# Scores of a windowed attention by halves of the queries, on quarters of the matrix array

## The chip, the cores and the metric

The kernel runs on one core of a Trainium2 chip. The metric is the device time of one execution in microseconds (us): 638.39 as the median of three runs before the change (638.38 to 638.89). Six actors matter. TensorE multiplies matrices, with a row PE for its matmuls and a row PEld for its weight loads. VectorE (DVE), ScalarE (ACT) and GpSimd (POOL) do the elementwise work, and SyncE (SP) issues the transfers from HBM. Each engine takes its instructions in the order in which they were written; semaphores join them.

## The reference, cut to what matters

Attention over 2 batches, 8 heads, 768 positions, heads 64 wide, where a query sees the first 4 positions and the last 128; then two layers over 1536 tokens:

```python
scores = scale * np.matmul(q, k.transpose(0, 1, 3, 2))
keep = is_sink | in_window          # pos < n_sink, or 0 <= rel < window
a = softmax(np.where(keep, scores, -1e9))
x = np.matmul(a, v)                 # then heads side by side: 1536 x 512
h = x @ w_in;  g = P(h) / (Q(h) + 1e-6);  x = g @ w_out      # rational layer
h = np.maximum(x @ w_in2, 0.0);  out = h * h @ w_out2         # squared relu
```

The weights come as 64-bit numbers, and the kernel takes them apart into 32-bit ones itself.

## The kernel before, in words

**Units and steps.** Attention runs over 12 units of 128 queries (6 blocks of positions in each of 2 batches). A unit has 8 heads, which go in 4 pairs; a pair is one step n of `step(n)`, so there are 48 steps. The two heads of a pair lie one above the other on the 128 partitions (64 each), so their score matmuls use the upper and the lower half of the array's rows.

**Scores.** `scores(n)` (L373 to L399) is called for two steps at once, every second step. A block of queries after the first of its batch (10 of the 12 units) needs the keys of its own block and of the one before. `keys` holds four slots of 136 columns: 128 keys of a block and 8 sink keys. For each head one matmul (L382) of 64 rows, 128 queries and 2 x 136 = 272 columns writes a bank of PSUM. In the profile each such 32-bit matmul is two instructions, so a call for two steps is eight of them (x8). The first block of a batch has 128 columns instead. VectorE then replaces the part of the own block that lies ahead of the query by the block before (`copy_predicated`, L387), adds the mask and takes the maximum (L394, tile `ns`, running maximum `nmax`). ScalarE takes the exponential into `pe` (L411) and adds it up into `rs`.

**Behind the scores.** Step n also transposes the probabilities of step n-2 (L431), copies them out of PSUM (`pc`, L439, ScalarE) and splits them by the diagonal (GpSimd, `ph`). It multiplies those of step n-4 by the values (`pv`, L471, tile `O`). Once a unit the probabilities of the sinks are gathered (`sk`), transposed (`sinks_t`, L454), cast to `st` (L457 on ScalarE, L458 on VectorE) and multiplied by the sink values (L478, L479), after which VectorE scales the unit's result to `x` (L482). `sums` turns `rs` into its reciprocal. `xt` transposes `x` (L353) and splits it in two parts (L497, L498). Between these, VectorE takes weights apart (L241, L247, L253).

**Zeros.** `fill(d, m)` issues m matmuls of zeros, 512 columns wide (L512), whose result nobody reads. `NW0` (14) stand at the start, and `DENSE` says how many stand ahead of the scores of some steps: 22 more, 36 in all.

**Order.** The order of each engine is the order in which `step` calls these functions; nothing rearranges it. The last four steps are laid between the first slots of the two layers, whose matmuls (L597, L676) fill the rest of the time. PSUM tiles rotate: `S` and `T` have two buffers each, `O` and `U` one.

Of the kernel before, what the change touches and what calls it, by code (L numbers as in the profile page):

```python
# [15 lines left out]
P = 128  # L16
SK = 8
# [1 line left out]
TWO32 = 4294967296.0  # L19
WS = 3  # L20
NW0 = 14
DENSE = {0: 4, 2: 4, 4: 3, 6: 3, 24: 2, 26: 2, 28: 2, 30: 2}
QP = 1.0 + 1e-6

LEAST = 2.0 ** -15 * 1.125
# [12 lines left out]
def kernel(  # L38
# [24 lines left out]
    UPC = CT // P  # L63
    scale = 1.0 / float(D) ** 0.5
    BS = P + SK
    NS = 4

    cst = ctx.enter_context(tc.tile_pool(name="cst", bufs=1))
    ctx.enter_context(tc.manual_schedule())
# [33 lines left out]
    def setup_first(m_0):  # L103
        ta, tb = [
            wr.tile([P, DM, 2], I32, tag="wr", name="su", bufs=NWR).rearrange("p n t -> p (n t)") for _ in range(2)
        ]
        it, it2 = ta[:, 0:2 * P], ta[:, 2 * P:3 * P]
        rel, col = ta[:, 4 * P:6 * P].bitcast(F32), ta[:, 6 * P:7 * P].bitcast(F32)
        win, snk, tmp, ge = (
            tb[:, a:b].bitcast(F32) for a, b in ((0, 2 * P), (2 * P, 3 * P), (3 * P, 4 * P), (4 * P, 6 * P))  # L110
        )
        rf, neg = tb[:, 6 * P:6 * P + 4].bitcast(F32), tb[:, 6 * P + 4:6 * P + 6].bitcast(F32)
        nc.gpsimd.iota(it, pattern=[[-1, 2 * P]], base=P, channel_multiplier=1)
        nc.gpsimd.iota(it2, pattern=[[1, P]], base=0, channel_multiplier=0)
        nc.vector.tensor_copy(rel, it)
        nc.vector.tensor_copy(col, it2)
        nc.vector.tensor_scalar(out=ge, in0=rel, scalar1=0.0, scalar2=None, op0=ALU.is_ge)
        nc.vector.tensor_copy(rf, raw)
        rv = rf.rearrange("p (j w) -> p j w", w=2)
        nc.vector.tensor_scalar(out=neg, in0=rv[:, :, 0], scalar1=0.0, scalar2=TWO32, op0=ALU.is_lt, op1=ALU.mult)  # L120
        nc.vector.scalar_tensor_tensor(out=nw, in0=rv[:, :, 1], scalar=TWO32, in1=neg, op0=ALU.mult, op1=ALU.add)
        nc.vector.tensor_tensor(out=nw, in0=nw, in1=rv[:, :, 0], op=ALU.add)
        yield
        window = lambda x: nc.vector.scalar_tensor_tensor(
            out=win[:, x], in0=rel[:, x], scalar=nw[:, 1:2], in1=ge[:, x], op0=ALU.is_lt, op1=ALU.mult
        )
        window(slice(P, 2 * P))
        nc.vector.scalar_tensor_tensor(
            out=tmp, in0=col, scalar=nw[:, 0:1], in1=win[:, P:], op0=ALU.is_lt, op1=ALU.max
        )  # L130
        addm(m_0, tmp)
        yield
        window(slice(0, P))
        nc.vector.tensor_scalar(out=snk[:, 0:SK], in0=col[:, 0:SK], scalar1=nw[:, 0:1], scalar2=None, op0=ALU.is_lt)
        yield rel, win, snk, tmp

    def setup_rest(rel, win, snk, tmp, m_1, m_2, tri):
        def addm_s(dst, src):
            nc.scalar.activation(out=dst, in_=src, func=ACTF.Identity, scale=BIG, bias=nbig)

        nc.vector.tensor_scalar(out=tri, in0=rel[:, P:], scalar1=0.0, scalar2=None, op0=ALU.is_lt)
        nc.gpsimd.tensor_tensor(out=tmp, in0=win[:, 0:P], in1=win[:, P:], op=ALU.add)
        nc.gpsimd.tensor_tensor(out=win[:, P:P + SK], in0=snk[:, 0:SK], in1=win[:, 0:SK], op=ALU.subtract)
        yield
        addm_s(m_1[:, 0:P], tmp)
        nc.scalar.activation(out=win[:, P:P + SK], in_=win[:, P:P + SK], func=ACTF.Relu)
        addm_s(m_1[:, P:], win[:, P:P + SK])
        yield
        addm_s(m_2[:, 0:P], tmp)
        addm_s(m_2[:, P:], snk[:, 0:SK])  # L150

    def setup_moe():
        nc.scalar.mul(out=na, in_=ab[:, 0:4], mul=-1.0)
# [138 lines left out]


    def attention(ap, extra):
        keys = ap.tile([P, NPR, NS, BS], F32, name="keys")
        m_0 = ap.tile([P, P], F32, name="m_0")
        m_1, m_2 = (ap.tile([P, 160], F32, name=f"m_{j}")[:, 0:BS] for j in (1, 2))
        tri = ap.tile([P, P], I32, name="tri")
# [3 lines left out]
        def load(u, what="qkv"):  # L302
            b, i = divmod(u, NB)
            for nm, src in (("q", q), ("k", k)):
                if nm in what:
                    t = keys[:, :, u % NS, 0:P] if nm == "k" else ap.tile([P, NPR, P], F32, name="qr", bufs=3)
                    nc.sync.dma_start(
                        out=t, in_=src[b, :, :, i * P:(i + 1) * P].rearrange("(r e) d t -> (e d) r t", e=2)
                    )
                    ld[u, nm] = t  # L310
            if "v" in what:
                t = ap.tile([P, H, D], F32, name="vr", bufs=5)
                nc.sync.dma_start(out=t, in_=v[b, :, i * P:(i + 1) * P, :].rearrange("h p d -> p h d"))
                ld[u, "v"] = t
# [42 lines left out]

        def sink_keys(u):
            nc.gpsimd.tensor_copy(
                keys[:, :, :, P:], keys[:, :, u % NS, 0:SK].unsqueeze(2).to_broadcast([P, NPR, NS, SK])  # L360
            )

        def geom(u):

            i, s = u % NB, u % NS
            if i == 0:
                return slice(s, s + 1), P, m_0, 0, None
            m = m_1 if i == 1 else m_2
            if s == 0:
                return slice(0, NS, NS - 1), BS, m, 0, BS  # L370
            return slice(s - 1, s + 1), BS, m, BS, 0

        def scores(n):  # L373
            u, pr = divmod(n, NPR)
            slots, bw, mask, co, po = geom(u)
            w = bw if po is None else 2 * bw
            t = ps_s()
            d = [t[:, e] for e in range(2)]
            fill(d[0], DENSE.get(n, 0))
            for e in range(2):  # L380
                s = slice(D * e, D * e + D)
                nc.tensor.matmul(  # L382
                    d[e][:, 0:w].rearrange("p (j n) -> p j n", n=bw),
                    lhsT=ld[u, "q"][s, pr, :], rhs=keys[s, pr, slots, 0:bw], start=True, stop=True,
                )
            if po is not None:
                nc.vector.copy_predicated(  # L387
                    out=t[:, :, co:co + P], mask=tri.unsqueeze(1).to_broadcast([P, 2, P]), data=t[:, :, po:po + P]
                )
            ns = []  # L390
            for e in range(2):
                ix = u * H + 2 * pr + e
                t = ap.tile([P, 160], F32, name="ns", bufs=6)
                nc.vector.tensor_tensor_reduce(  # L394
                    out=t[:, 0:bw], in0=d[e][:, co:co + bw], in1=mask, scale=-scale, scalar=3.0e38,
                    op0=ALU.add, op1=ALU.min, accum_out=nmax[:, ix:ix + 1],
                )
                ns.append(t)
            kps[n] = ns  # L399

        def expo(n):
            u, pr = divmod(n, NPR)
            w = geom(u)[1]
            if pr == 0:
                pe_t[u] = ap.tile([P, NPR, 2, BS], F32, name="pe", bufs=2)
                rs_t[u] = ap.tile([P, 32], F32, name="rs", bufs=3)[:, 0:H]
            rs, t = rs_t[u], pe_t[u][:, pr]
            ns = kps.pop(n)
            for e in range(2):
                ix = u * H + 2 * pr + e  # L410
                nc.scalar.activation(  # L411
                    out=t[:, e, 0:w], in_=ns[e][:, 0:w], func=ACTF.Exp, scale=-1.0,
                    bias=nmax[:, ix:ix + 1], accum_out=rs[:, 2 * pr + e:2 * pr + e + 1],
                )
            pr_t[n] = t

        def sinks(n):
            u = n // NPR
            t = pe_t.pop(u)
            if u % NB and n % NPR == NPR - 1:  # L420
                sk[u] = ap.tile([P, 2, H, SK], F32, name="sk", bufs=2)
                nc.gpsimd.tensor_copy(
                    sk[u], t[:, :, :, P:].rearrange("p r e s -> p (r e) s").unsqueeze(1).to_broadcast([P, 2, H, SK])
                )

        def trans(n):
# [1 line left out]
            t = pr_t.pop(n)  # L428
            d = ps_t(tail=n >= NP - 2)
            for e in range(2):  # L430
                nc.tensor.transpose(d[:, e * P:(e + 1) * P], t[:, e, 0:P], ident)  # L431
            h = mp.tile([P, CT], F32R, tag=("gh", "gl")[n % 2], name="ph", bufs=2)
            h = h.bitcast(F32).rearrange("p (j e t) -> p j e t", j=2, e=2)
            dv = d[:, 0:2 * P].rearrange("p (e t) -> p e t", e=2)
# [83 lines left out]
        load(0, "v")  # L518
        load(1, "v")
        nc.sync.dma_start(out=ab, in_=coefs.partition_broadcast(P))  # L520
        fill(ps_t("T"), NW0)
        masks = setup_first(m_0)
        next(masks)
        next(masks)
# [2 lines left out]
        def step(n):  # L527
# [4 lines left out]
            if n == 0:  # L532
                scores(0)
                scores(1)
                rest = setup_rest(*next(masks), m_1, m_2, tri)
                next(rest)
                sink_keys(0)
            elif n % 2 == 0 and n < NP:
                scores(n)
                scores(n + 1)  # L540
            if 0 < n < 4:
                next(rest, None)
            if n == 2:
# [9 lines left out]
                trans(n - 2)  # L553
            if 0 <= n - 1 < NP and pr == 0:
                sinks(n - 1)
            if (n >= 6 and pr == 2 and n < NP) or n == NP + 1:
                sinks_t(n // 4 - 1)
                sums(n // 4 - 1)
            if 12 <= n <= NP and pr == 0:
                xt(n // 4 - 3)  # L560
            if n == NP + 1:
                xt(NU - 2)
            if 0 <= n - 4 < NP:
                pv(n - 4)
            if n == NP - 2:
                g1(0)
            if pr == 2 and u % NB == 0 and 0 < u < NU:
# [522 lines left out]
```

## Time and profile before

| | us |
|---|---|
| median of three runs | 638.39 |
| profiled execution | 638.53 |
| its span, first to last instruction | 636.8 |
| TensorE busy in the span | 625.2 (98%) |
| VectorE, ScalarE, GpSimd busy | 423.3, 356.6, 339.0 |

The span is 1.7 us shorter than the profiled execution's own time. Attention takes about the first 112 us of it. A busy matmul row counts from the start of a matmul to its modelled end, so that matmuls overlap; what TensorE's work costs is read from the distances between starts, as the chain of waits gives them.

### The profile page before, as it was taken

The page shows a single profiled execution, that of the slowest core. Times are in us where ns is not written, and L with a number is a line of the kernel's source. Part 1 is how long each engine was busy: PE and PEld are TensorE (multiplying, and loading weights), DVE is VectorE, ACT ScalarE, POOL GpSimd, SP SyncE. Part 2 cuts the span into 40 slices and gives each one's busy share as a digit, 9 for nine tenths or more (in the row PEclk, how much of TensorE's full clock was granted, in tenths as well). Part 3 has the DMA queues.
Part 4 walks back from the last instruction along what each step waited for, and adds up shares of the span by engine and source line. Part 5 has one row for each costly group of instructions (what it writes and reads, how often), then busy time and mean ns, then how long its engine had stood idle before and what let it go on. Part 6 is the DMA issues. An engine that isn't in the chain of part 4 may idle for free.

```text
span 636.8 us, 9037 instructions
## 1 busy us (share of the span) xinstructions
PE 625.2 (98%) x3060; PEld 514.7 (81%) x3060; DVE 423.3 (66%) x862; ACT 356.6 (56%) x772; POOL 339.0 (53%) x343
## 2 busy tenths in 40 slices
PE   8999999999999999999999999999999999999995
PEld 6788787888888888888888888888888888888884
DVE  4887884679888888777677779869594433441321
ACT  4777877778888788697778633333242222222220
POOL 3666865667767577586567557444443132222221
PEclk9999999999999999999999999999999999999999
DMA  8846820033223233201111148737556264420101
GB/s 214 251 128 180 226 71 31 1 99 100 83 84 100 66 100 99 67 33 34 33 46 55 35 136 259 245 115 243 191 166 231 69 221 123 173 76 1 66 1 72
DMA packets 64373, 72.03 MB, mean 113 GB/s; under 512 B 15424, under 2 KB 55360, under 8 KB 64320
## 3 DMA queue, kind: packets, MB, share of 16 engines
q1 hardware_dynamic: 64176, 71.38, 36.1%
q8 instruction: 26, 0.43, 0.3%
q14 instruction: 27, 0.22, 0.1%
q10 hardware_dynamic: 144, 0.00, 0.0%
HBM read 68.23 MB, written 3.15 MB: 112 GB/s over the span
## 4 chain that ended last, share of the span: by engine, by line
PE 92%; DVE 3%; ACT 3%; issue 1%; POOL 0%; DVEq 0%; ACTq 0%
PE s L676 41%; PE T L597 34%; PE U L597 7%; PE O L471 3%; PE s L382 3%; PE T L431 1%; DVE ns L394 1%; PE T L512 1%; ACT pe L411 1%; PE s L512 1%; PE O L478 1%; DVE s L387 0%; ACT pc L439 0%; ACT xf L497 0%; PE O L479 0%
## 5 line engine op out<-in xcount | busy, mean ns | idle before, releaser
L597 PE MATMUL T<-xh,w 128*128 128x512 f32 x640 | 210.4, 390 | 0.0
L659 POOL TENSOR_TENSOR gl<-g,gh 128x512 fp32r<-128x512 f32 x48 | 62.1, 1294 | 158.0 <-ACT gh L658 157.9
L597 PEld LDWEIGHTS T<-xh,w 128*128 128x128 f32 x640 | 120.2, 188 | 25.0
L676 PE MATMUL s<-gh,w 128*128 128x512 f32 x384 | 126.3, 390 | 0.0
L597 PE MATMUL T<-xl,w 128*128 128x512 f32 x320 | 124.5, 389 | 0.0
L676 PE MATMUL s<-w,gh 128*128 128x512 f32 x384 | 118.1, 389 | 0.0
L618 POOL TENSOR_TENSOR t<-t,ah 128x512 f32<-128x512 f32 x48 | 62.3, 1297 | 41.8 <-ACT t L615 35.9
L275 POOL TENSOR_TENSOR w<-wx,w 128x512 fp32r<-128x512 f32 x64 | 82.7, 1292 | 3.2 <-ACT w L274 3.0
L676 PEld LDWEIGHTS s<-gh,w 128*128 128x128 f32 x384 | 72.1, 188 | 15.0
L676 PEld LDWEIGHTS s<-w,gh 128*128 128x128 f32 x384 | 72.1, 188 | 14.9
L659 POOL TENSOR_TENSOR gl<-t,gh 128x512 fp32r<-128x512 f32 x48 | 62.3, 1297 | 38.0 <-ACT gh L658 35.1
L658 ACT CAST gh<-g 128x512 fp32r<-128x512 f32 x48 | 29.9, 623 | 82.4 <-PE s L676 77.0
L676 PE MATMUL s<-gl,w 128*128 128x512 f32 x192 | 74.7, 389 | 0.0
L676 PE MATMUL s<-w,gl 128*128 128x512 f32 x192 | 74.7, 389 | 0.0
L597 PEld LDWEIGHTS T<-xl,w 128*128 128x128 f32 x320 | 60.1, 188 | 12.3
L647 DVE SCALAR_TENSOR_TENSOR t<-t,U 128x512 f32<-128x512 f32 x48 | 33.0, 687 | 35.9 <-ACT U L644 35.6
L658 ACT CAST gh<-t 128x512 fp32r<-128x512 f32 x48 | 29.8, 622 | 37.6 <-DVE t L651 29.3
L632 DVE TENSOR_TENSOR g<-r,T 128x512 f32<-128x512 f32 x32 | 21.8, 683 | 42.8 <-ACT r L622 42.8
L622 ACT ACTIVATE r<-T 128x512 f32<-128x512 f32 x32 | 19.1, 598 | 53.2 <-PE T L597 53.1
L471 PE MATMUL O<-vr,ph 128*128 128x64 f32 x352 | 44.6, 268 | 0.2 <-DVE x L482 0.2
L471 PEld LDWEIGHTS O<-vr,ph 128*128 128x128 f32 x352 | 43.3, 192 | 0.6 <-POOL vm L337 0.5
L274 ACT CAST w<-wx 128x512 fp32r<-128x512 f32 x64 | 39.5, 618 | 7.7 <-DVE wx L253 7.2
(152 smaller groups left out, 1065.9 us busy)
## 6 DMA issues: line engine op xcount, KB each, us to landing
wr<-in_w_in_dram SPq DMA_DIRECT2D x54, 512.0 KB, 3.7
wr<-in_w_out_dram SPq DMA_DIRECT2D x52, 512.0 KB, 3.9
qr<-in_q_dram SPq DMA_DIRECT2D x12, 256.0 KB, 4.4
keys<-in_k_dram SPq DMA_DIRECT2D x12, 256.0 KB, 4.3
vr<-in_v_dram SPq DMA_DIRECT2D x12, 256.0 KB, 4.6
wr<-in_v_dram SPq DMA_DIRECT2D x6, 512.0 KB, 4.6
out_dram<-part SPq DMA_DIRECT2D x12, 256.0 KB, 2.0
vsc<-in_v_dram SPq DMA_DIRECT2D x4, 16.0 KB
```

What stands on the lines that cost most here:

```text
L274: nc.scalar.copy(out=t[:, 0], in_=xf)
L275: nc.gpsimd.tensor_tensor(out=t[:, 1], in0=xf, in1=t[:, 0].bitcast(F32), op=ALU.subtract)
L382: nc.tensor.matmul(d[e][:, 0:w].rearrange("p (j n) -> p j n", n=bw), lhsT=ld[u, "q"][s, pr, :], rhs=keys[s, pr, slots, 0:bw], start=True, ...
L471: nc.tensor.matmul(o[:, h * D:(h + 1) * D], lhsT=pt[:, j, e], rhs=ld[u - 1 + j, "v"][:, h, :], start=(h == 0 and j == (i == 0)), stop=Fals ...
L597: nc.tensor.matmul(h, lhsT=wi[a][:, kk * P:(kk + 1) * P], rhs=(xh, xl)[b][c][:, kk, :], start=(kk == 0 and a + b == 0), stop=(kk == KD - 1 ...
L618: nc.gpsimd.tensor_tensor(out=t, in0=t, in1=ah, op=ALU.mult)
L622: nc.scalar.activation(out=r, in_=h, func=ACTF.Relu)
L632: nc.vector.tensor_tensor(out=g, in0=st.pop(k), in1=h, op=ALU.mult)
L647: nc.vector.scalar_tensor_tensor(out=t, in0=t, scalar=QP, in1=r0, op0=ALU.add, op1=ALU.mult)
L658: nc.scalar.copy(out=gh, in_=g)
L659: nc.gpsimd.tensor_tensor(out=gl, in0=g, in1=gh.bitcast(F32), op=ALU.subtract)
L676: nc.tensor.matmul(acc[L, g, c][m], lhsT=lh, rhs=rh, start=(f == f0 and a + b == 0), stop=(f == f1 and a == 1),)
```

## The change

The score matmul of 128 queries and 272 columns becomes two of 64 queries and 200 columns. The first half of the queries takes columns 0 to 199 of the 272, the second half 64 to 263; each writes its own 64 partitions of the same bank. `keys` has six slots, one for each block of a batch, so that a block and the one before always lie side by side. The merged part of the scores is now [8 sinks, 128 keys], so the masks and the rows of `pe` turn round: a row of `pe` is 160 long and ends with its 128 keys. The two PSUM tiles of the scores are taken once (`ss`) and used in turn. The zeros at the start go into these two tiles. Those of steps 0 and 2 stand behind the scores instead of ahead of them, five and four, in the `T` tiles, and the others are gone: 23 zeros in all. `sinks_t` and `sums` are called one step sooner, at the end of the step and ahead of the next scores. One copy in the set-up (`rf`) is gone.

```diff
-DENSE = {0: 4, 2: 4, 4: 3, 6: 3, 24: 2, 26: 2, 28: 2, 30: 2}
+DENSE = {0: 5, 2: 4}
...
-        nc.vector.tensor_copy(rf, raw)
-        rv = rf.rearrange("p (j w) -> p j w", w=2)
+        rv = raw.rearrange("p (j w) -> p j w", w=2)
...
-        keys = ap.tile([P, NPR, NS, BS], F32, name="keys")
+        keys = ap.tile([P, NPR, NB, BS], F32, name="keys")
...
-            t = ps_s()
+            t = ss[n % 2]
             d = [t[:, e] for e in range(2)]
-            fill(d[0], DENSE.get(n, 0))
-            for e in range(2):
-                s = slice(D * e, D * e + D)
-                nc.tensor.matmul(
-                    d[e][:, 0:w].rearrange("p (j n) -> p j n", n=bw),
-                    lhsT=ld[u, "q"][s, pr, :], rhs=keys[s, pr, slots, 0:bw], start=True, stop=True,
-                )
...
+                for g in range(2):
+                    for e in range(2):
+                        s, r = slice(D * e, D * e + D), slice(hf * g, hf * g + BS + hf)
+                        nc.tensor.matmul(
+                            d[e][hf * g:hf * g + hf, r], lhsT=ld[u, "q"][s, pr, hf * g:hf * g + hf],
+                            rhs=keys[s, pr, i - 1:i + 1, :].rearrange("p i n -> p (i n)")[:, r],
+                            start=True, stop=True,
+                        )
...
-                pe_t[u] = ap.tile([P, NPR, 2, BS], F32, name="pe", bufs=2)
+                pe_t[u] = ap.tile([P, NPR, 2, ROW], F32, name="pe", bufs=2)
...
-                    out=t[:, e, 0:w], in_=ns[e][:, 0:w], func=ACTF.Exp, scale=-1.0,
+                    out=t[:, e, ROW - w:], in_=ns[e][:, 0:w], func=ACTF.Exp, scale=-1.0,
...
-        fill(ps_t("T"), NW0)
+        ss = [ps_s() for _ in range(2)]
+        for j in range(NW0):
+            fill(ss[j // 2 % 2][:, j % 2], 1)
...
+                if n in DENSE:
+                    fill(ps_t("T"), DENSE[n])
...
-            if (n >= 6 and pr == 2 and n < NP) or n == NP + 1:
-                sinks_t(n // 4 - 1)
-                sums(n // 4 - 1)
...
             if 0 <= n - 4 < NP:
                 pv(n - 4)
+            if 5 <= n <= NP + 1 and pr == 1:
+                sinks_t(n // 4 - 1)
+                sums(n // 4 - 1)
```

On TensorE, at the start of the program, before (wz are the zeros, keys and qr the scores' operands, ident and pe the transposes of the probabilities):

```order
L512 MATMUL T<-wz 128x512 x14
L512 MATMUL s<-wz 128x512 x4
L382 MATMUL s<-keys,qr 128x128 x4
L512 MATMUL s<-wz 128x512 x4
L382 MATMUL s<-keys,qr 128x128 x4
L431 MATMUL T<-ident,pe 128x128 x4
L512 MATMUL s<-wz 128x512 x3
L382 MATMUL s<-keys,qr 128x272 x4
```

and the same place now:

```order
L510 MATMUL s<-wz 128x512 x14
L371 MATMUL s<-keys,qr 128x128 x4
L510 MATMUL T<-wz 128x512 x5
L371 MATMUL s<-keys,qr 128x128 x4
L510 MATMUL T<-wz 128x512 x4
L429 MATMUL T<-ident,pe 128x128 x4
L380 MATMUL s<-keys,qr 64x200 x8
```

The first scores stand behind 14 zeros instead of 18, and those of step 4 directly behind the transposes.

On TensorE, steps 12 to 15 (the fourth unit), before, where sk are the sinks' probabilities and st, with vsh and vsl, the sinks' part of the product:

```order
L382 MATMUL s<-keys,qr 128x272 x4
L431 MATMUL T<-ident,pe 128x128 x2
L454 MATMUL T<-ident,sk 128x128
L471 MATMUL O<-vr,ph 128x64 x4
L431 MATMUL T<-ident,pe 128x128 x2
L471 MATMUL O<-vr,ph 128x64 x4
L478 MATMUL O<-vsh,st 128x512
L479 MATMUL O<-vsl,st 128x512
```

and now:

```order
L452 MATMUL T<-ident,sk 128x128
L380 MATMUL s<-keys,qr 64x200 x8
L429 MATMUL T<-ident,pe 128x128 x2
L469 MATMUL O<-vr,ph 128x64 x4
L429 MATMUL T<-ident,pe 128x128 x2
L469 MATMUL O<-vr,ph 128x64 x4
L476 MATMUL O<-vsh,st 128x512
L477 MATMUL O<-vsl,st 128x512
```

The transpose of the sinks went ahead of the scores of two steps, so six blocks of work lie between it and its use instead of three.

On VectorE, at the end of the same unit, before (st and rs are the sinks' cast and the reciprocal, x the unit's result):

```order
L387 COPY_PREDICATED s<-tri,s 128x2x128
L394 ISA ns,nmax<-s,m_107 128x136
L394 ISA nmax 128x1
L458 TENSOR_TENSOR st<-T,st 64x128
L491 RECIPROCAL rs<-rs 128x8
L482 TENSOR_TENSOR x<-O,rs 128x512
```

and now:

```order
L252 SCALAR_TENSOR_TENSOR wx<-wr,U 128x512
L456 TENSOR_TENSOR st<-T,st 64x128
L489 RECIPROCAL rs<-rs 128x8
L240 TENSOR_SCALAR U<-wr 128x512
L385 COPY_PREDICATED s<-tri,s 128x2x128
L392 ISA ns,nmax<-s,m_107 128x136
```

The cast of the sinks and the reciprocal moved from behind the score work of two steps to ahead of it.

## Rows read from the trace of the kernel before

**Rows 1.** The page's 40 slices: busy tenths of TensorE, its granted clock.

```profile
PE   8999999999999999999999999999999999999995
PEclk9999999999999999999999999999999999999999
```

**Rows 2.** Busy time by stage; the first line names the columns.

```profile
core 0: us, PE busy (x) PEld busy (x) DVE busy (x) ACT busy (x) POOL busy (x), PEclk, DMA share, GB/s
12.92:16.16 3.24, 3.24 (x24) 2.41 (x23) 1.83 (x10) 3.18 (x17) 1.13 (x2) 1.00 0.98 317
...
28.02:52.68 24.66, 24.22 (x192) 20.13 (x192) 20.81 (x80) 19.75 (x79) 17.57 (x35) 1.00 0.55 151
52.68:60.57 7.89, 7.89 (x69) 6.83 (x68) 4.86 (x23) 6.31 (x25) 4.73 (x9) 1.00 0.63 172
...
67.25:92.01 24.76, 24.43 (x190) 19.91 (x190) 20.84 (x84) 20.85 (x85) 19.94 (x39) 1.00 0.53 148
92.01:112.19 20.18, 19.43 (x129) 16.51 (x129) 10.71 (x33) 14.31 (x43) 11.44 (x20) 1.00 0.09 27
```

**Rows 3.** The chain of waits, in order of time: start, us, what.

```profile
44.44 1.12 PE s L382 x8
...
46.36 0.84 PE O L471 x8
```

**Rows 4.** Timeline, narrow windows: score matmuls (PE), their loads (PEld).

```profile
44.37 0.50 PE L382 MATMUL s<-keys,qr 64*128 64x272 f32 x2
44.70 0.62 PE L382 MATMUL s<-keys,qr 64*128 64x272 f32 x4
44.93 0.62 PE L382 MATMUL s<-keys,qr 64*128 64x272 f32 x4
...
44.37 0.30 PEld L382 LDWEIGHTS s<-keys,qr 64*128 64x128 f32 x4 [0.36 <-issue]
44.48 0.19 PEld L382 LDWEIGHTS s<-keys,qr 64*128 64x128 f32 x2
```

**Rows 5.** The chain: zeros (L512), and scores of 128 columns; VectorE's first score work.

```profile
7.08 0.92 PE s L512 x4
...
8.47 0.29 DVE L394 CUSTOM_DVE_ANT_0 ns<-s,m 128x128 f32<-128x128 f32 x1 [1.50 <-PE s L382]
...
12.28 0.71 PE s L512 x3
15.48 0.75 PE s L512 x3
52.29 0.46 PE s L512 x2
52.75 0.65 PE s L382 x8
56.11 0.52 PE s L512 x2
60.18 0.46 PE s L512 x2
```

**Rows 6.** Issue of the first keys, and the keys' time to landing.

```profile
1.33 0.49 SPq L307 DMA_DIRECT2D keys<-in_k_dram  x1
...
DMA to landing us min/median/max: 4.2/4.3/7.3
```

**Rows 7.** Who waited for whom, 12 to 112 us: total, times, longest.

```profile
PEld O L478 <- DVE st L458: 1.1, 3, 0.6
...
PE O L478 <- DVE st L458: 0.4, 1, 0.4
```

**Rows 8.** Timeline of TensorE where attention ends.

```profile
109.86 0.27 PE L454 MATMUL s<-ident,sk 128*128 128x128 f32 x1
110.89 0.66 PE L353 MATMUL s<-ident,x 128*128 128x128 f32 x4 [0.75 <-ACT pc L439]
```

**Rows 9.** Loads of the probabilities for their transposes: ns min/median/max.

```profile
L431 PEld LDWEIGHTS T<-ident,pe x90: 137/142/199, 10.9 to 97.0; 128*128 128x128 f32 x90
```

More of the change, by code (lines that the diff above doesn't have):

```diff
@@ L65 @@
     BS = P + SK
-    NS = 4
+    ROW = 160
     cst = ctx.enter_context(tc.tile_pool(name="cst", bufs=1))
@@ L111, in setup_first @@
         )
-        rf, neg = tb[:, 6 * P:6 * P + 4].bitcast(F32), tb[:, 6 * P + 4:6 * P + 6].bitcast(F32)
+        neg = tb[:, 6 * P:6 * P + 2].bitcast(F32)
         nc.gpsimd.iota(it, pattern=[[-1, 2 * P]], base=P, channel_multiplier=1)
@@ L144, in setup_rest @@
         yield
-        addm_s(m_1[:, 0:P], tmp)
+        addm_s(m_1[:, SK:], tmp)
         nc.scalar.activation(out=win[:, P:P + SK], in_=win[:, P:P + SK], func=ACTF.Relu)
-        addm_s(m_1[:, P:], win[:, P:P + SK])
+        addm_s(m_1[:, 0:SK], win[:, P:P + SK])
         yield
-        addm_s(m_2[:, 0:P], tmp)
-        addm_s(m_2[:, P:], snk[:, 0:SK])
+        addm_s(m_2[:, SK:], tmp)
+        addm_s(m_2[:, 0:SK], snk[:, 0:SK])
     def setup_moe():
@@ L305, in load @@
                 if nm in what:
-                    t = keys[:, :, u % NS, 0:P] if nm == "k" else ap.tile([P, NPR, P], F32, name="qr", bufs=3)
+                    t = keys[:, :, u % NB, 0:P] if nm == "k" else ap.tile([P, NPR, P], F32, name="qr", bufs=3)
                     nc.sync.dma_start(
@@ L359, in sink_keys @@
             nc.gpsimd.tensor_copy(
-                keys[:, :, :, P:], keys[:, :, u % NS, 0:SK].unsqueeze(2).to_broadcast([P, NPR, NS, SK])
+                keys[:, :, :, P:], keys[:, :, u % NB, 0:SK].unsqueeze(2).to_broadcast([P, NPR, NB, SK])
             )
[L363 to L371, printed above, removed]
@@ L373, in scores @@
         def scores(n):
             u, pr = divmod(n, NPR)
-            slots, bw, mask, co, po = geom(u)
-            w = bw if po is None else 2 * bw
-            t = ps_s()
+            i = u % NB
+            t = ss[n % 2]
             d = [t[:, e] for e in range(2)]
-            fill(d[0], DENSE.get(n, 0))
-            for e in range(2):
-                s = slice(D * e, D * e + D)
-                nc.tensor.matmul(
-                    d[e][:, 0:w].rearrange("p (j n) -> p j n", n=bw),
-                    lhsT=ld[u, "q"][s, pr, :], rhs=keys[s, pr, slots, 0:bw], start=True, stop=True,
-                )
@@ L386, in scores @@
-            if po is not None:
+            if i == 0:
+                mask, co, bw = m_0, 0, P
+                for e in range(2):
+                    s = slice(D * e, D * e + D)
+                    nc.tensor.matmul(
+                        d[e][:, 0:P], lhsT=ld[u, "q"][s, pr, :], rhs=keys[s, pr, 0, 0:P], start=True, stop=True
+                    )
+            else:
+                mask, co, bw = (m_1 if i == 1 else m_2), P, BS
+                hf = P // 2
+                for g in range(2):
+                    for e in range(2):
+                        s, r = slice(D * e, D * e + D), slice(hf * g, hf * g + BS + hf)
+                        nc.tensor.matmul(
+                            d[e][hf * g:hf * g + hf, r], lhsT=ld[u, "q"][s, pr, hf * g:hf * g + hf],
+                            rhs=keys[s, pr, i - 1:i + 1, :].rearrange("p i n -> p (i n)")[:, r],
+                            start=True, stop=True,
+                        )
@@ L387, in scores @@
                 nc.vector.copy_predicated(
-                    out=t[:, :, co:co + P], mask=tri.unsqueeze(1).to_broadcast([P, 2, P]), data=t[:, :, po:po + P]
+                    out=t[:, :, BS:BS + P], mask=tri.unsqueeze(1).to_broadcast([P, 2, P]), data=t[:, :, 0:P]
                 )
@@ L402, in expo @@
             u, pr = divmod(n, NPR)
-            w = geom(u)[1]
+            w = BS if u % NB else P
             if pr == 0:
-                pe_t[u] = ap.tile([P, NPR, 2, BS], F32, name="pe", bufs=2)
+                pe_t[u] = ap.tile([P, NPR, 2, ROW], F32, name="pe", bufs=2)
                 rs_t[u] = ap.tile([P, 32], F32, name="rs", bufs=3)[:, 0:H]
@@ L422, in sinks @@
                 nc.gpsimd.tensor_copy(
-                    sk[u], t[:, :, :, P:].rearrange("p r e s -> p (r e) s").unsqueeze(1).to_broadcast([P, 2, H, SK])
+                    sk[u], t[:, :, :, ROW - BS:ROW - P].rearrange("p r e s -> p (r e) s").unsqueeze(1).to_broadcast([P, 2, H, SK])
                 )
@@ L430, in trans @@
             for e in range(2):
-                nc.tensor.transpose(d[:, e * P:(e + 1) * P], t[:, e, 0:P], ident)
+                nc.tensor.transpose(d[:, e * P:(e + 1) * P], t[:, e, ROW - P:], ident)
             h = mp.tile([P, CT], F32R, tag=("gh", "gl")[n % 2], name="ph", bufs=2)
@@ L540, in step @@
                 scores(n + 1)
+                if n in DENSE:
+                    fill(ps_t("T"), DENSE[n])
             if 0 < n < 4:
```

## The prediction

> **What bounds the kernel now.** I read the page's slices first. TensorE is at nine tenths or more from the second slice to the last but one, at the full granted clock [rows 1], so a microsecond taken off TensorE's path is taken off the end, as long as no other engine takes its place. The change lies in attention, the first 112 us, so I read that by stage. In 28 to 52.7 us TensorE is busy 24.2 of 24.7 us, VectorE 20.8 and ScalarE 19.8; in 67 to 92 the two stand at 20.8 of 24.8 [rows 2]. TensorE leads, with two engines some 16% behind it. The chain of waits says the same: it is a run of TensorE pieces (scores 1.12 us, products 0.84) broken by stretches on ScalarE and VectorE. Of the 20 calls for two steps of 272 columns, 13 lie on the chain as a whole piece of 1.12 us like those of [rows 3], and one by half. In the other six or so the chain runs over VectorE or ScalarE, and faster scores buy nothing at once.
>
> **Scores (20 calls).** The eight instructions of a call go in four rounds of two, the two heads at the same time: the first two start at 44.37, the next at 44.70 and the third two at 44.93 (each row tells the start of the first of its matmuls), so a round in the middle takes 0.23 us [rows 4]. The call of 272 columns takes 1.12 us, that of 128 columns 0.65 [rows 3, 5]. So a column costs (1.12 - 0.65) / 144 = 3.3 ns over four rounds, and what doesn't depend on columns is 0.65 - 128 x 3.3 ns = 0.23 us. A call of 200 columns in four rounds, now of four instructions each, is then 0.23 + 200 x 3.3 ns = 0.89 us: 0.23 less, 4.7 us over 20 calls.
>
> This stands on the four quarters running at once. The trace shows the two row halves doing it and no column halves, so the bounds are wide. If the two column halves run one after the other, there are eight rounds: 0.23 + 400 x 3.3 ns = 1.55 us, 0.43 more, 8.6 over 20 calls. Below, with the weight load halved too (0.11 us between the first and the second pair of loads [rows 4], so some 0.05), a call is 0.84. I take 0.89, since the nearest row, the pair of row halves, shows no loss at all from sharing.
>
> The Trainium skill ("TensorE: Matmul & The Clock Gate", Part 3: Packing small matmuls) has a figure that is less kind: three column tiles gave 2.38 times the speed of one, 79% of full. By that share, as an estimate, a call would take about 1.06 us and the term would be 1.2 us instead of 4.7; no run here shows column tiles yet.
>
> What follows when TensorE needs 0.47 us less for a unit of four steps: in 28 to 52.7 us six calls save 1.4, and VectorE's 20.8 us are then 89% of 23.3. That still fits, but the waits grow. I credit the 13.5 calls on the chain, 3.2 us, and give back 0.6 to VectorE and ScalarE: **2.6 us**.
>
> **Zeros (36 to 23).** The first scores waited for 18 zeros; now 14. The four in between are 0.92 us on the chain [rows 5]. What could be late instead: the first keys, issued at 1.33 and landed some 4.3 to 5 us later [rows 6], so by about 6.3, while 14 zeros end at 7.1; and the mask, but VectorE sat idle for 1.50 us before 8.47, waiting for the scores alone [rows 5]. So 0.9 us. The copy `rf` lies in that idle time: nothing. The zeros of steps 4 and 6 are 0.71 and 0.75 us on the chain [rows 5], but ScalarE is busy 3.18 of 3.24 us between them [rows 2], so it becomes late there, and I credit 1.0 of the 1.46. Those moved behind the scores of steps 0 and 2 run while TensorE waits for the first exponentials. In steps 24 to 28 three pieces of 0.46, 0.52 and 0.46 are on the chain [rows 5] and the pair of step 30 is not; ScalarE is busy 6.31 of 7.89 us there [rows 2]. I credit 0.8 of 1.44. Together **2.7 us** (at most 3.8).
>
> **Sinks one step sooner.** TensorE waited 1.5 us in all, four times, for the cast `st` [rows 7]; with six blocks between its transpose and its use that goes. But `st` now stands ahead of the score work on VectorE, and waits there for ScalarE's half of the cast. Where ScalarE is behind, the two `copy_predicated` and four maxima queued behind it start later, and through them the exponentials. I credit **0.4 us** (bounds: 1.5 gained, and as much lost, if the wait only goes over from TensorE to VectorE at a place that counts).
>
> **Where attention ends.** The transposes of `x` waited 0.75 us for a copy that frees their buffer of the scores' tiles, with the sinks' transpose in between [rows 8]. By the new order `xt` comes before `sinks_t`, takes the buffer that was freed earlier, and the sinks' transpose is the one behind the last copy, after the products. ScalarE is the busy engine there, so **0.5 us** of 0.75.
>
> **At nothing.** Rows of `pe` at 160: a load for a transpose takes 142 ns, and 137 at best [rows 9]; were those of all 48 steps at their best, under 0.5 us. Six slots instead of four: two copies of sink keys grow by half, on GpSimd, which is not on the chain there; keys may be loaded sooner, but no wait for them stands in the chain. The new masks are as many instructions as the old ones.
>
> **Sum.** 2.6 + 2.7 + 0.4 + 0.5 = 6.2 us. The profiled execution took 638.53 us by its own time, 0.14 over the median of the runs, so 638.5 - 6.2 = **632.3 us**. Since TensorE has no waits from 112 us on until the last slice [rows 1], I expect nothing of it given back later.
>
> **Rivals.**
>
> *The weight loads stick out.* The skill's same section says that a weight load overlaps a matmul in flight only where its rows differ. In the trace the second pair of loads starts at 44.48, on the same two row halves as the matmuls that started at 44.37 and last 0.5 us [rows 4], so the row of before speaks against it. But two quarters of one row half may share the path by which weights come. As a mechanism here: each of the four rounds waits for the load of one or of both quarters of a row half, 0.05 us each (half of the 0.11 between loads), so that a call takes 0.89 + 0.2 or + 0.4 = 1.09 or 1.29. On 13.5 calls that is 0.4 gained or 2.3 lost; with the 3.6 us of zeros, sinks and end it gives 634.5 to 637.2, in the middle **635.9**.
>
> *VectorE and ScalarE take it back.* If the chain moves to them as soon as TensorE is quicker (both are at 84% in 67 to 92 us [rows 2], and `st` ties them closer together), the scores give 1 us, the zeros 1.9, the rest nothing: **635.6**. For it: six calls already off the chain. Against: at 89% they still fit.
>
> *The column halves run one after the other* (the other side). Place: the score matmuls; price: 0.43 us a call. On 13.5 calls of the chain that is 5.8, on all 20 it is 8.6; less the 3.6 us of the other parts that is 2.2 to 5.0 slower, **642**. It decides from a call of 1.30 us on, where 20 calls lose as much as the rest wins. For it: no row shows two column groups at once. Against: the row halves do share the array.
>
> *The clock falls.* With 13 fewer zeros TensorE has more gaps early and in steps 24 to 31. It is at 1.00 in every stage of [rows 2]; were it at half in one such stage of 8 us, TensorE would need up to 8 us more there: about 637. TensorE keeps four fifths of its work in these stages, so I hold it unlikely.
>
> **How the numbers follow.** The forecast (four quarters at once, 4 to 9 us faster) 64%; loads stick out 11%; VectorE and ScalarE take it back 9%; halves one after the other 11%; clock and anything else 5%. The forecast alone spans 629 to 635; the range goes up to 637.5, to hold the two rivals near 636 and their spread, and leaves out the slower one: 629.0 to 637.5. A measurement of this kernel tells 0.2%, 1.3 us, from no change. The forecast is faster, and so is most of the next two: 0.81 faster, 0.08 within, 0.11 slower.
>
> **What would show it.** Right: eight-round calls don't appear; sixteen score instructions start in four groups of four about 0.17 us apart, and a call takes 0.85 to 0.9 us on the chain; the first scores start near 7.0 instead of 7.93; no wait of L476 for `st`; the first slot without attention starts some 6 us sooner. Wrong: groups of two in eight rounds; a granted clock under 1.00 after 7 us; VectorE waiting for ScalarE at `st`, with a chain that runs mostly over the two; TensorE waiting for weights in the layers behind.

## The result, and the profile after

The changed kernel takes 630.53 us (median of four runs, 630.33 to 632.53), against 638.38 in the same comparison: 7.85 us faster by the medians, where 6.2 was forecast. The ratio is 0.9886 with a 95% interval of 0.9863 to 0.9909, which is 7.3 us (5.8 to 8.7). Its profiled execution took 630.33 us, with a span of 628.6. Ten of the 53 executions of kernels with both the new scores and the early sinks (in e2, e7, e9 and e12) took 6 to 11 us longer at a mean granted clock of 0.972 to 0.985 instead of 0.991 or more; no profile holds one, so where the clock was lost stays open, and e9, with five of the ten, can't be read.

The page's slices of after; they answer to [rows 1]:

```profile
PE   8999999999999999999999999999999999999995
DVE  4987874698888988787587879689594423541321
ACT  5888878678787888697778533333242221222210
PEclk9999999999999999999999999999999999999998
```

TensorE is still at nine tenths or more in all slices but the first and the last, and its clock holds through attention. So the time was won by handing TensorE less work and by letting it wait less, not by another engine taking over. The windows of after, in two of the stretches of [rows 2] (the work in them is not quite the same work, since all of it is earlier now):

```profile
core 0: us, PE busy (x) PEld busy (x) DVE busy (x) ACT busy (x) POOL busy (x), PEclk, DMA share, GB/s
28.02:52.68 24.66, 24.58 (x251) 20.35 (x247) 21.11 (x86) 21.26 (x85) 19.50 (x38) 1.00 0.64 179
...
67.25:92.01 24.76, 24.60 (x244) 19.61 (x243) 21.27 (x87) 20.54 (x80) 18.94 (x36) 1.00 0.40 119
```

TensorE went from 24.22 to 24.58 and from 24.43 to 24.60: fuller, not emptier, though its score work shrank. That is the first hint that a wait went away too.

Six narrow windows of after's timeline on one call of the scores, four of the matmuls and two of their loads. A row shows the instructions in flight, with the start of the first; they answer to [rows 4]:

```profile
42.85 0.57 PE L380 MATMUL s<-keys,qr 64*64 64x200 f32 x8
43.07 0.52 PE L380 MATMUL s<-keys,qr 64*64 64x200 f32 x8
43.24 0.52 PE L380 MATMUL s<-keys,qr 64*64 64x200 f32 x8
43.41 0.35 PE L380 MATMUL s<-keys,qr 64*64 64x200 f32 x4
...
42.85 0.15 PEld L380 LDWEIGHTS s<-keys,qr 64*64 64x64 f32 x4
42.85 0.21 PEld L380 LDWEIGHTS s<-keys,qr 64*64 64x64 f32 x8
```

There are four rounds, not eight. They start at 42.85, 43.07, 43.24 and 43.41, with four matmuls each. The last three are 0.17 us apart. Eight loads are done within 0.21 us of the start of the first, four of them while the first four matmuls are in flight, so the later rounds do not wait for weights. The first distance is 0.22 us, 0.05 more than the others. Before it was 0.33 against 0.23, 0.10 more [rows 4]. That fits first matmuls that wait for their own load, which has half as many columns now.

After's chain of waits over one pair of steps that is TensorE's own work, [rows 3] before:

```profile
24.25 0.84 PE s L380 x16
25.08 0.37 PE T L429 x2
25.45 0.44 PE T L352 x4
25.89 0.84 PE O L469 x8
26.73 0.23 PE T L429 x2
26.96 0.84 PE O L469 x8
27.80 0.12 PE T L452
27.91 0.84 PE s L380 x16
```

The call went from 1.12 to 0.84, and this half of a unit takes 3.66 us from score to score. The other half has the two products with the sinks, 0.28 and 0.24, in place of 0.44 and 0.12, so a unit at TensorE's own pace is 7.3 us. With the old call it would be 0.56 more, 7.86.

Last, who waited for whom, 12 us to the end of attention. The first fence is after, the second a row of before that [rows 7] does not have:

```profile
PEld s L380 <- DVE nmax L392: 6.6, 15, 0.8
...
PE s L380 <- DVE nmax L392: 1.7, 5, 0.4
...
DVE x L480 <- PE O L477: 5.7, 6, 3.5
...
DVE st L456 <- ACT st L455: 2.8, 5, 1.4
```

```profile
DVE x L482 <- PE O L479: 9.6, 9, 3.5
```

TensorE's wait for `st` is gone. VectorE's wait for the sinks' product shrank from 9.6 us, nine times, to 5.7, six times; one piece of 3.5, at the end of attention, is the same in both, so the rest went from 6.1 to 2.2. And a wait has grown, of the scores for VectorE's maxima, which release the scores' buffer. Most of its 6.6 us is the loads' row standing idle while matmuls still run; TensorE's matmuls wait 1.7 us for it.

### The profile page after: what moved, and what is told of

It is laid out like the page before. It is cut to its first block, busy times and chain, and to the rows that moved or that the text cites. A ratio compares the mean times of both kernels' runs of the same rounds, so it can differ in the third digit from the quotient of the medians.

```text
span 628.6 us, 9308 instructions
## 1 busy us (share of the span) xinstructions
PE 617.5 (98%) x3207; PEld 507.7 (81%) x3207; DVE 422.6 (67%) x861; ACT 357.2 (57%) x772; POOL 339.2 (54%) x343
## 4 chain that ended last, share of the span: by engine, by line
PE 91%; DVE 4%; ACT 3%; DMA 1%; issue 0%; POOL 0%; SPq 0%; DVEq 0%; ACTq 0%
PE s L679 42%; PE T L600 34%; PE U L600 7%; PE O L469 4%; PE s L380 2%; PE T L429 1%; ACT pe L409 1%; DVE ns L392 1%; DMA keys<-in_k_dram 1%; DVE s L385 1%; PE O L476 0%; DVE wx L252 0%; PE O L477 0%; PE T L352 0%; DVE U L246 0%
## 5 line engine op out<-in xcount | busy, mean ns | idle before, releaser
L409 ACT ACTIVATE pe<-ns,nmax 128x136 f32<-128x136 f32 (+1 forms) x96 | 38.3, 403 | 9.3 <-DVE nmax L392 9.0
```

The lines of the kernel that those rows point to most:

```text
L409: nc.scalar.activation(out=t[:, e, ROW - w:], in_=ns[e][:, 0:w], func=ACTF.Exp, scale=-1.0, bias=nmax[:, ix:ix + 1], accum_out=rs[:, 2 * p ...
```

## The experiments

The theories were: the new scores do most of it; the order of the sinks does much more than credited; the parts add up or they do not. Each part was taken out of after, and each was put into before alone. All times are medians beside runs of before on the same chip (638.18, 638.64 and 637.74 us in the three comparisons). After was not run again beside them, so what a part is worth by removal is a difference between two comparisons, good to some 2 us by their intervals.

**e1, after with whole scores.**

```diff
-                for g in range(2):
-                    for e in range(2):
...
-                            d[e][hf * g:hf * g + hf, r], lhsT=ld[u, "q"][s, pr, hf * g:hf * g + hf],
...
+                for e in range(2):
...
+                        d[e][:, 0:2 * BS], lhsT=ld[u, "q"][s, pr, :],
...
```

> The changed kernel with the score matmuls of the ten two-block units put back to 128 queries and 272 columns; zeros, order, slots and rows stay new. In the changed kernel's trace a score call takes 0.84 us on the chain where it took 1.12. Theory A (the predicted mechanism, sized a little larger): most of the 20 calls count, 0.28 x 13.5 to 20 = 3.8 to 5.6, less what VectorE and ScalarE take back, so this kernel is 3 to 5 us slower than the changed one: 633.5 to 635.5. Theory B (VectorE and ScalarE take it back, the zeros and the order carry the 7.9 us): under 1.5 us slower than the changed one, 630.5 to 632.

632.80 us, ratio 0.9912 (0.9898 to 0.9927). So by the medians the scores are worth 2.3 us in the finished kernel; 2.6 were credited. The chain of e1 from 28 to 46 us is TensorE alone, at 1.12 a call, as in these rows of it:

```profile
32.43 1.12 PE s L378 x8
...
36.38 1.12 PE s L378 x8
...
40.29 1.12 PE s L378 x8
```

Two pairs of steps take 7.86 us: TensorE's own pace with the old call, and no wait left.

**e2, after with all 22 zeros back ahead of the scores.**

```diff
-DENSE = {0: 5, 2: 4}
+DENSE = {0: 4, 2: 4, 4: 3, 6: 3, 24: 2, 26: 2, 28: 2, 30: 2}
...
+            fill(d[0], DENSE.get(n, 0))
...
-                fill(ps_t("T"), DENSE[n])
...
-                if n in DENSE:
-                    fill(ps_t("T"), DENSE[n])
```

> The changed kernel with the 22 zeros of the steps where they stood before (4, 4, 3, 3, then 2 four times), ahead of the scores; the 14 first ones stay in the scores' tiles. Theory A: 2 to 2.7 us slower than the changed kernel, 632.5 to 633.3, with the zeros of steps 4, 6 and 24 to 30 back on the chain. Theory B: 3.5 us or more slower, 634 or above.

632.97 us, ratio 0.9936 (0.9908 to 0.9964): 2.4 us by the medians, against a credit of 2.7.

**e3, after with the sinks at their old place.**

```diff
+            if (n >= 6 and pr == 2 and n < NP) or n == NP + 1:
+                sinks_t(n // 4 - 1)
+                sums(n // 4 - 1)
...
-            if 5 <= n <= NP + 1 and pr == 1:
-                sinks_t(n // 4 - 1)
-                sums(n // 4 - 1)
```

> The changed kernel with the sinks' transpose, its cast and the reciprocal of the sums called where they were before (one step later, ahead of the products). Theory A: 0.4 to 1 us slower than the changed kernel (TensorE's waits for the cast, 1.5 us before, come back at four places or so), 631 to 631.5; the wait of VectorE for ScalarE at this cast (2.8 us in the changed kernel's trace) goes. Theory B: 1.5 us or more slower. Third: faster than the changed kernel, if those 2.8 us of VectorE cost more than the waits they replaced.

634.93 us, ratio 0.9949 (0.9937 to 0.9962): the move that was credited 0.4 us (and 0.5 at the end of attention, which this edit undoes too) is worth 4.4, the largest part of all. The timeline of e3 at the end of a unit, TensorE and VectorE:

```profile
39.65 0.29 DVE L392 CUSTOM_DVE_ANT_0 ns<-s,m 128x136 f32<-128x136 f32 x1
...
39.99 0.29 DVE L456 TENSOR_TENSOR st<-T,st 64x128 fp32r<-64x128 f32 x1
...
40.34 0.50 PE L476 MATMUL O<-vsh,st 128*128 128x512 f32 x1 [0.72 <-DVE st L456]
40.67 0.40 PE L477 MATMUL O<-vsl,st 128*128 128x512 f32 x1
41.00 0.91 PE L380 MATMUL s<-keys,qr 64*64 64x200 f32 x16
41.11 0.69 DVE L480 TENSOR_TENSOR x<-O,rs 128x512 f32<-128x512 f32 x1 [0.59 <-PE O L477]
```

The same place in after:

```profile
38.49 0.47 PE L476 MATMUL O<-vsh,st 128*128 128x512 f32 x1
...
38.80 0.40 PE L477 MATMUL O<-vsl,st 128*128 128x512 f32 x1
...
39.13 0.97 PE L380 MATMUL s<-keys,qr 64*64 64x200 f32 x16
...
39.17 0.29 DVE L392 CUSTOM_DVE_ANT_0 ns<-s,m 128x136 f32<-128x136 f32 x1
...
39.39 0.69 DVE L480 TENSOR_TENSOR x<-O,rs 128x512 f32<-128x512 f32 x1
```

In e3 the work goes from VectorE (`st`) to TensorE (L476, L477) and back to VectorE (`x`). First TensorE stands still for 0.72 us, then VectorE for 0.59. In after `st` was made long before, the products end while VectorE is at its maxima, and `x` follows on them directly. The waits of e3 have VectorE's side of it nine times, 9.7 us, as before, and three rows of TensorE's own:

```profile
DVE x L480 <- PE O L477: 9.7, 9, 3.6
...
PE s L380 <- DVE nmax L392: 2.0, 5, 0.4
...
PE T L429 <- ACT pc L437: 1.4, 3, 0.6
PE O L476 <- DVE st L456: 1.4, 2, 0.7
```

From the scores of step 4 to the last pair, TensorE is idle for 5.3 of 81.2 us in e3 and for 2.2 of 77.4 in after. Of the three waits of TensorE only the first is in after too (1.7 us). The wait for `st` is 1.4 us, and the wait for ScalarE's copies `pc` is as much. That the copies come late because VectorE's maxima do is argued from the order of the work and was not tested.

**e4, after with zeros and sinks as in before: the new scores alone** (the edits of e2 and e3 together).

> Only the scores by quarters, with their slots, masks and rows: zeros and the sinks' call both as before. Theory A: 3 to 5 us faster than the kernel before, 633.5 to 635.5. Theory B: at most 1.5 us faster, 637 or above.

637.06 us, ratio 0.9982 (0.9973 to 0.9990): 1.1 us. This is the new scores with all that belongs to them (slots, masks, rows, fixed tiles, `rf`), where e1 takes out the small matmuls alone. The scores save 5.6 us of TensorE's work (20 x 0.28) in both e4 and after, but with the old order much of it turns into waiting. From the scores of step 4 to the last pair TensorE is idle for 4.2 of 81.8 us in e4, where before it was 1.9 of 82.9. Its named waits in e4 are 1.4 us for ScalarE's copies, 1.4 for `st` and 0.8 for the maxima.

**e5, before with the early sinks alone** (e3's edit the other way round).

> The kernel before with one edit: the sinks' transpose, its cast and the reciprocal of the sums called at the end of the step before, as in the changed kernel. Theory C, formed on the first four runs (putting this call back cost 4.4 us): before, once a unit VectorE ends its score work with the cast, TensorE multiplies by it (0.5 and 0.24 us), and VectorE idles until that product is there before it can scale the unit's result; 6 of those 9.6 us of VectorE's wait lie in eight units. Alone it then gives 3 to 4.5 us: 633.7 to 635.2. Theory D: it pays only because the scores are faster; alone at most 1.5 us: 636.7 or above.

636.10 us, ratio 0.9961 (0.9947 to 0.9974): 2.5 us, in between the numbers expected. Its chain from 28 to 46 us is all TensorE, and its wait for the products with the sinks fell to 6.2 us in five pieces:

```profile
30.87 1.12 PE s L382 x8
...
38.73 1.12 PE s L382 x8
```

```profile
DVE x L482 <- PE O L479: 6.2, 5, 3.5
```

A unit takes 7.86 us, TensorE's own pace with the old call. So in this stretch the move alone can win no more: the next gain has to come out of TensorE's work, and the scores are that.

**e6, after with only `sums` at its old place.**

```diff
 if 5 <= n <= NP + 1 and pr == 1:
     sinks_t(n // 4 - 1)
-    sums(n // 4 - 1)
```

> The changed kernel with the reciprocal of the sums called one step later again, the sinks' transpose and cast where the change put them. Theory C: the cast is what TensorE and then VectorE waited for, the reciprocal is not, so within 0.7 us of the changed kernel, 630 to 631.2. Rival: the reciprocal (0.2 us on VectorE, behind 0.3 us on ScalarE) belongs to the round trip as much; then 1.5 us or more slower.

630.33 us, ratio 0.9872 (0.9857 to 0.9887), the same as after: what counts is `sinks_t`, the sinks' transpose and the cast `st`, not the reciprocal. The transpose and the cast were not moved apart.

**e7, after without the nine zeros of steps 0 and 2** (`DENSE = {}`).

> The changed kernel without the nine zeros of steps 0 and 2; the 14 first ones stay. If they only fill time in which TensorE waits for the first exponentials: within 0.7 us of the changed kernel, 629.9 to 631.2. If they hold up the transposes behind them: 0.7 to 2 us faster. If TensorE's granted clock falls without them: 1 us or more slower, and a clock row under 1.00 between 7 and 20 us.

631.14 us, ratio 0.9882 (0.9864 to 0.9900), no different from after: no cost of the nine is seen. In after's profile the chain runs over the other engines there, from 7.0 to 22.6 us. Whether the nine help to hold the clock is open.

**e8, after without `copy_predicated`** (it leaves out the merging of the two blocks' scores).

```diff
-                nc.vector.copy_predicated(
-                    out=t[:, :, BS:BS + P], mask=tri.unsqueeze(1).to_broadcast([P, 2, P]), data=t[:, :, 0:P]
-                )
```

> The changed kernel without the copy_predicated of the scores (40 instructions of 0.43 us on VectorE and the time to start each), so that the own block's scores ahead of the query are not replaced by those of the block before and its output is not the reference's. If VectorE is what holds attention in the changed kernel (TensorE waits 8.3 us in all for its score tiles): 3 us or more faster, 627.5 or below. If TensorE bounds it: at most 1.5 us faster, 629 or above.

628.38 us, ratio 0.9844 (0.9830 to 0.9859): with 40 copies off VectorE the kernel is 2.2 us faster, in between the numbers expected. VectorE's busy time in the same window falls from 21.11 to 16.59, TensorE's stays:

```profile
28.02:52.68 24.66, 24.62 (x242) 20.87 (x240) 16.59 (x76) 21.28 (x86) 18.69 (x35) 1.00 0.67 187
```

So VectorE holds back about 2 us of after, about as much as the 1.7 us that TensorE's matmuls wait for the maxima there.

**e9, e6 with the weights' conversions ahead of `st`.**

```diff
 if 5 <= n <= NP + 1 and pr == 1:
+    extra(n, True)
     sinks_t(n // 4 - 1)
```

> A try at a better version: the changed kernel with the sums' reciprocal late, and at the end of the step VectorE's share of the weights' conversion issued ahead of the sinks' cast instead of behind it. VectorE waited 3.1 us in five places for ScalarE's half of that cast; 0.7 us conversions now lie in front. If these waits hold up the scores behind them: 0.5 to 2 us faster than the changed kernel, 628.5 to 630. If TensorE bounds what is left (its own work is about 7.3 us of the 7.4 to 7.9 of a unit): within 0.5 us of the kernel with the late sums, 630.3.

633.17 us, 630.34 to 638.58 in twelve runs, ratio 0.9948 (0.9917 to 0.9979): inconclusive. Its best runs are about as long as those of e6 and of after, so no gain is seen in it.

**e10, before with the new zeros alone.**

```diff
-fill(d[0], DENSE.get(n, 0))
...
+if n in DENSE:
+    fill(ps_t("T"), DENSE[n])
```

> The kernel before with one edit: the zeros of the steps as in the changed kernel (five and four behind the scores of steps 0 and 2, the rest gone). Theory A (the terms stand by themselves): 2 to 2.7 us faster than the kernel before, as much as putting them back cost the changed one (2.4). Theory C (what one edit gives is held by the engine that is next): the zeros of steps 24 to 30 give little while VectorE's round trip stands, the head 1 to 1.5: 1 to 1.8 us faster.

636.31 us, ratio 0.9973 (0.9962 to 0.9983): 1.4 us by the medians (1.1 to 2.4 by the interval). That is less than the 2.4 by removal, but the interval does not part the two.

**e11, after with rows of 136** (`ROW = BS`).

> The changed kernel with rows of the probabilities of 136 instead of 160 elements, so that the 128 keys of a row start at element 8 of it. Every theory here: within 0.5 us of the changed kernel, loads for the transposes at a median of 142 ns in both. If the alignment of the row counts: a longer median load or exponential, and 1 us or more slower.

631.21 us, ratio 0.9898 (0.9884 to 0.9911): the same as after. The loads of the probabilities, [rows 9] before, are the same in after and in e11, in this order:

```profile
L429 PEld LDWEIGHTS T<-ident,pe x90: 137/142/198, 9.9 to 89.3; 128*128 128x128 f32 x90
...
L429 PEld LDWEIGHTS T<-ident,pe x90: 137/142/199, 10.7 to 90.1; 128*128 128x128 f32 x90
```

**e12, after with only the last call of the sinks ahead of `xt`, as before.**

```diff
+            if n == NP + 1:
+                sinks_t(n // 4 - 1)
+                sums(n // 4 - 1)
...
-            if 5 <= n <= NP + 1 and pr == 1:
+            if 5 <= n < NP and pr == 1:
```

> The changed kernel with the last call of the sinks' transpose, where attention ends, ahead of the transposes of x as it was before; all other units new. By the trace the wait of 0.75 us of TensorE for the last copy comes back: 0.5 to 0.9 us slower than the changed kernel, 631 to 631.5, with a TensorE gap ahead of the transposes of x. If ScalarE bounds that place anyway: within 0.3 us of it.

631.61 us, ratio 0.9917 (0.9887 to 0.9946): too wide for half a microsecond. The timeline of e12's TensorE where attention ends has the gap of [rows 8] again:

```profile
101.99 0.27 PE L452 MATMUL s<-ident,sk 128*128 128x128 f32 x1
103.02 0.66 PE L352 MATMUL s<-ident,x 128*128 128x128 f32 x4 [0.76 <-ACT pc L437]
```

And in after:

```profile
102.09 0.60 PE L352 MATMUL s<-ident,x 128*128 128x128 f32 x4
102.52 1.00 PE L469 MATMUL O<-vr,ph 128*128 128x64 f32 x8
103.36 0.28 PE L452 MATMUL s<-ident,sk 128*128 128x128 f32 x1
103.97 0.50 PE L600 MATMUL T<-xh,w 128*128 128x512 f32 x1 [0.33 <-DVE t L629]
```

From the last pair of scores to the end it is 540.95 us in e12 and 540.46 in after, one profile each.

## Why the prediction was nearly right, and where it was not

The score starts in the timelines show how the parts work together. Five pairs of steps (12 to 22) and six (32 to 44), us:

| kernel | 12 to 22 | 32 to 44 |
|---|---|---|
| before | 20.18 | 24.76 |
| scores alone (e4) | 19.74 | 25.36 |
| sinks alone (e5) | 19.65 | 24.08 |
| after | 18.67 | 23.59 |
| after without the copies (e8) | 18.56 | 22.24 |
| TensorE's own work, 3.65 a pair | 18.3 | 21.9 |

In the first stretch the scores alone gain 0.4, the sinks alone 0.5, and the whole change 1.5. In the second the scores alone lose 0.6, the sinks alone gain 0.7, the whole change 1.2. In that loss TensorE's idle time goes from 0.3 to 2.0 us, of which 0.8 is for ScalarE's copies, 0.7 for `st` and 0.3 for the maxima. Before, TensorE and VectorE took turns at the end of some of the units: shorter scores mostly made TensorE wait longer, and a better order only brought it to its own pace of 7.86 a unit.

By removal the scores, the sinks and the zeros are worth 2.3, 4.4 and 2.4, in sum 9.1; alone 1.1, 2.5 and 1.4, in sum 5.0. The measured 7.85 lies between. Within the profiles, from the scores of step 4 to the last pair, the three are worth 2.0, 3.8 and 0.8 by removal, 1.1, 2.2 and 1.0 alone, and the whole change 5.6. These distances leave out the start, where executions of one kernel differ. So scores and sinks need each other; the zeros there give as much either way.

- **Scores.** The mechanism was right: four quarters at once, rounds of 0.17, a call of 0.84 (0.89 forecast, 0.84 the bound with the load halved too). Of 5.6 us of work 2.3 reached the end (2.6 credited). The estimate of 1.06 a call, worked out from the share of three column tiles in the Trainium skill ("TensorE: Matmul & The Clock Gate", Part 3: Packing small matmuls), is not borne out here: the call took 0.84, and no loss by sharing is seen. That figure of the Trainium skill is for tiles of 32 columns, which no run here has.
- **Zeros.** 2.4 by removal, 1.4 alone, 2.7 credited. The first scores start at 6.44, not 7.0:

```profile
1.12 4.91 PE L510 MATMUL s<-wz 128*128 128x512 f32 x14 [1.12 <-DVE nbig L505]
6.44 0.71 PE L371 MATMUL s<-keys,qr 64*128 64x128 f32 x8 [0.41 <-DMA keys<-in_k_dram]
```

The same 14 zeros took 5.96 us in before's profile and 4.91 here, so the keys, which landed at 6.30 as the prediction had it, are now late by 0.41. Over all the profiles the first scores start at 6.1 to 7.2 behind 14 zeros and at 7.6 to 8.3 behind 18. Of the 1.5 us between 7.93 and 6.44, about 0.85 is the four zeros less, as forecast, and some 0.65 is of that execution.

- **Sinks one step sooner: the step that failed.** It was priced by TensorE's wait for `st` alone, 1.5 us [rows 7], and credited 0.4. With the end of attention it is worth 4.4 by removal and 2.5 alone, beyond the upper bounds of the two terms together (1.5 and 0.75). What it overlooked is the way back: VectorE, with ScalarE the second busiest engine there [rows 2], stood 9.6 us waiting for the sinks' product, and 3.9 of that went with the earlier cast. TensorE's direct wait for `st`, 1.4 in e3, was about the size that was read; the rest came, as far as the waits of e3 tell, by way of the other two engines. The fear that `st` would wait for ScalarE at the head of the score work came true in 2.8 us, and did not decide.
- **End of attention.** 0.5 credited; the gap of 0.75 is gone, 0.5 by the distance to the end. The run times don't settle it.
- **At nothing.** Rows of 160: nothing (e11). Six slots, masks and `rf` were not tried singly; no wait for keys after the first stands in after's chain.
- **Given back.** 0.6 was set off for VectorE and ScalarE. e8 says about 2 us, for VectorE's part, and the wait of L380 for `nmax` is where it shows.
- **Rivals.** Loads that stick out and halves one after the other: dead, by the four rounds 0.17 us apart. VectorE and ScalarE take it back: true for the scores alone (e4), undone by the new order in the whole change. The clock: 1.00 in attention in the profile, from its first record at 4.20 us on.

So the total of 6.2 came near 7.85 with one term, the sinks with the end, too small by 1.6 to 3.5 us. By removal the others were about right; by the edits alone, scores and zeros were credited some 1.4 too much each. That the sum came out so near is in part luck: it added terms that do not stand by themselves, and what it credited too freely made up for what it overlooked. The last pair of scores starts at 88.16 instead of 95.84, 7.7 us sooner where some 6 were forecast (with the 0.65 of that execution in it), and behind attention TensorE has no wait that gives any of it back.

## What to carry to other kernels

When two engines run nearly full, price a moved instruction by the waits of both, and follow a round trip (VectorE to TensorE and back) to where it ends: the row that mattered here was the second engine's. An edit's worth alone and by removal can differ by a factor of two, so test both before saying what it is worth. Matmuls of a quarter of the array ran four at a time here (0.17 us a round), so that fewer columns were time saved on TensorE; how much of it reaches the end depends on the engine that frees their buffer.

## What was not expected of the hardware

- Four matmuls of 64 rows and 64 columns ran together at no visible loss: 0.17 us a round of 200 columns, against 0.23 us a round of two for 272 [rows 4]. A column costs 0.85 ns in a round in both cases.
- Loads of 64x64 weights went in while matmuls on the same rows were in flight, eight within 0.21 us.
- The same 14 zeros at the start took 4.91 us in one profiled execution and 5.96 in another. In all 14 profiles the zeros behind the first start 0.43 us apart to begin with and 0.23 apart later, and the change falls where the trace has its first record of the granted clock (1.00): at 4.20 us in after, at 6.50 in before, at 4.0 to 7.2 over all. Ahead of that record the trace says nothing of the clock, and the 1.00 that the views print there is no reading. Nearly twice the distance fits the lower of the clock's two levels, 1.2 instead of 2.4 GHz, but no record shows it.
